# Sink exponentials of a windowed attention: from two fp16 parts in the DMA transposes to one fp32 block turned on TensorE

## The chip, the cores and the metric

The kernel runs on one core of a Trainium2 chip. The metric is the device time of one execution in microseconds (us), the median over several runs. The profile is one more execution, recorded instruction by instruction; its times count from its first instruction.

## What is computed

Three layers follow each other. The change is in the first, an attention with a window of 128 keys and 4 sink keys that every query may see; 2 batches, 8 heads, 768 positions, 64 values per head:

```
scores = scale * np.matmul(q, k.transpose(0, 1, 3, 2))
is_sink = pos[None, :] < int(n_sink)
in_window = (rel >= 0) & (rel < int(window))
scores = np.where(is_sink | in_window, scores, -1000000000.0)
a = np.exp(scores - np.max(scores, axis=-1, keepdims=True))
a = a / (np.sum(a, axis=-1, keepdims=True) + 1e-09)
return np.matmul(a, v).astype(np.float32)
```

Its output, 1536 rows of 512, goes through eight experts (two matrix products each, weighted by normalised gates) and then through a layer with `h * cos(h)`. These two fill most of the time.

## The kernel before

Products are made from fp16 pairs: a value x is stored as a high part `hi` and the rest `lo = x - hi`, and three matmuls give hi·hi, hi·lo and lo·hi.

**Units.** The attention is cut into 48 units, numbered k = 0 to 47: a batch (24 units each), one of four pairs of heads p, and one of six tiles i of 128 queries. Within a pair of heads, units are summed in groups that share one PSUM tile: two groups of three tiles for the first three pairs, three groups of two tiles for the last. Each unit passes through the engines like this:

- `scores(k)` (L533, TensorE): two fp32 matmuls, one per head. 260 columns are 128 keys of the tile before, 4 sink keys and 128 keys of the own tile (132 for the first tile). They go into one ring of four PSUM banks, so two units' scores fit.
- `top(k)` (L545, VectorE, two instructions and two reads of the maximum), then `nm` (L549, VectorE): mask, row maximum, and the bias of the exponential.
- `expo(k)` (L563, ScalarE) and `high(k)` (L574, ScalarE): exponentials, and their fp16 high part of the window's columns.
- `low(k)` (L579, GpSimd): the low part of the window's columns. The eight sink columns (two heads, four sinks) are split on VectorE: L582 makes the high part, L584, one unit later, the low part. They lie in block 0 of the unit's nine blocks of 128 columns.
- `turn(k)` (L589, queue of SyncE): a DMA transposes the nine blocks (five for the first tile).
- `values(k)` (L601, L606, TensorE): two matmuls of 130 columns with block 0 and the sinks' V in two parts (`vs`), then six or twelve matmuls of 65 columns with the other blocks.
- `norm(k)` at the end of a group (L615 to L618, VectorE).

**Order.** Every engine runs its instructions in the order in which the program issues them. That order is set by a hand-written table of ticks: `put(t, every, steps)` puts steps at ticks, `run(n)` issues those of tick n, and `late` holds steps for the start of the next tick. Unit k's scores are at tick 2k (2k+4 for the second batch), its `low` five ticks after, its `values` thirteen ticks after. Work that shares these ticks is placed by the `put` lines that the diff touches: loading V and splitting it (`prep_v`, L187, L189, L190), the sinks' V (`sinks`, L477 on TensorE and L478 on VectorE), loading and scaling the first expert's weights (`w_load`, `w1_split`, L170 for the maxima, L128 to L161 for the scale), and from tick 37 the turning of finished rows into the experts' operand (`x_operand`, L183, L184, L204 to L206, L212). The first batch's ticks end at 66; the second batch's 60 ticks are spread over the first expert's first pass.

Of the kernel before, what the change touches and what calls it, by code (L numbers as in the profile page):

```python
# [10 lines left out]
F32 = mybir.dt.float32  # L11
# [29 lines left out]
def kernel(  # L41
# [263 lines left out]
    def attention():  # L305
# [28 lines left out]
        a16s, ats = Ring(parts16[:, n] for n in range(3)), Ring(parts16[:, n] for n in range(3, 7))  # L334
        more = W2S[0].rearrange("p a b w -> p (a b w)")[:, 3 * 1792:3 * 1792 + 18 * 128].rearrange("p (n a w) -> p n a w", a=9, w=128)
# [4 lines left out]
        for b, home in ((0, HH), (1, W2S[1])):  # L340
            h = home.rearrange("p a b w -> p (a b w)")
            n, n2 = 2 * NP * NT * 2 * DV, 2 * NP * 2 * DV
            vh[b] = h[:, 0:n].rearrange("p (l a t g d) -> p l a t g d", l=2, a=NP, t=NT, g=2)
            vs[b] = h[:, n:n + n2].rearrange("p (l a g d) -> p l a g d", l=2, a=NP, g=2)
# [74 lines left out]
        rep = res.tile([128, 128], F16, name="rep")  # L419
        bm = res.tile([128, 2], F32, name="bm")  # L420
        b2 = res.tile([128, 2], F32, name="bm2")

        def sink_consts():
            for t in a16s.parts:
                nc.gpsimd.memset(t[:, 0, :], 0.0)
            nc.gpsimd.memset(rep, 0.0)
            r = rep[:, 0:4 * NS].rearrange("p (g s) -> p g s", s=NS)
            nc.gpsimd.memset(r, 1.0)
            sel(r, [(0, 1, [[0, 4], [-1, NS]]), (0, -1, [[0, 4], [1, NS]])], 0.0)
            for g, t in enumerate((bm, b2)):  # L430
                nc.gpsimd.memset(t, 1.0)
                o = 2 * g * NS
                sel(t, [(-o, 1, [[-NS, 2]]), (o + NS - 1, -1, [[NS, 2]])], 0.0)
            nc.gpsimd.tensor_tensor(out=bm, in0=bm, in1=b2, op=ALU.add)
# [5 lines left out]
        def prep_v(b, groups):  # L440
# [33 lines left out]
            def sinks(p):  # L474
                ps = ring["l"].next()[:, 0:4 * DV].rearrange("p (l g d) -> p l g d", l=2, g=2)
                for hl in range(2):
                    nc.tensor.matmul(ps[:, hl], rep, vh[b][:, hl, p, 0], start=True, stop=True)  # L477
                nc.vector.tensor_tensor(  # L478
                    out=vs[b][:, :, p], in0=ps, in1=bm[:, None, :, None].to_broadcast([128, 2, 2, DV]), op=ALU.mult)

            def sp(p):
                src = vt[:, p].rearrange("p t (g d) -> p t g d", g=2)
                split(vh[b][:, 0, p, :, :, 0:D], vh[b][:, 1, p, :, :, 0:D], src, sv[:, p:p + 1], by=BY[b][p])

            for n, g in enumerate(groups):
# [5 lines left out]
                for p in range(g.start, g.stop):  # L491
                    steps.append(lambda p=p: sp(p))
                    steps.append(lambda p=p: sinks(p))
            return steps + [ones_col]
# [27 lines left out]
        S_, A_, N_, a16_, at_, X_ = {}, {}, {}, {}, {}, {}  # L522
# [53 lines left out]
        def low(k):  # L576
# [3 lines left out]
            sk = a16_[k][:, 0, 0:4 * NS].rearrange("p (g h s) -> p g h s", g=2, h=2)  # L580
            asn = A.rearrange("p h b w -> p h (b w)")[:, :, 128:TW]
            nc.vector.tensor_copy(out=sk[:, 0], in_=asn)  # L582
            between.append(
                lambda: nc.vector.tensor_tensor(out=sk[:, 1], in0=asn, in1=sk[:, 0], op=ALU.subtract))  # L584

        def turn(k):
# [3 lines left out]
                out=at[:, 0:n], in_=a16_.pop(k)[:, 0:n].rearrange("p a w -> p (a w)"))  # L590

        def values(k):
# [3 lines left out]
            if u == 0:  # L596
                X_[b] = ring["x"].next()[:, 0:n * 2 * DV].rearrange("p (u g d) -> p u g d", u=n, g=2)
            xp = X_[b][:, u]
            nb = 2 if i else 1
            for vi in range(2):  # L600
                nc.tensor.matmul(  # L601
                    xp, at[:, 0, :], vs[b][:, vi, p], start=(vi == 0), stop=False)
            for h in range(2):
                for j in range(nb):
                    for ai, vi in ((0, 0), (0, 1), (1, 0)):
                        nc.tensor.matmul(  # L606
                            xp[:, h], at[:, 1 + 2 * nb * ai + h * nb + j, :], vh[b][:, vi, p, i - (nb - 1) + j, h],
                            start=False, stop=(h == 1 and j == nb - 1 and ai == 1))
# [99 lines left out]
        put(7, 0.5, wl1[:4])  # L708
        p0 = prep_v(0, (slice(0, 1), slice(1, NP)))
# [4 lines left out]
        put(4, 1, p0[-1:])  # L714
        put(8, 1, p0[3:4])
        put(6, 1.0, p0[4:7])
        put(10, 2, p0[7:9])
        put(12, 0.5, p0[9:-1:2])
        put(15, 2.5, p0[10:-1:2])
# [82 lines left out]
    def experts(before):  # L802
# [458 lines left out]
```

## Time and profile before

| | |
|---|---|
| median of three runs | 1353.39 us (1352.38 to 1355.0) |
| the profiled execution's own time | 1356.48 us |
| its span, first to last instruction | 1354.8 us |
| busy over the span: TensorE, VectorE, ScalarE, GpSimd | 94%, 66%, 51%, 47% |
| mean granted clock of TensorE | 0.972 of full speed |

The engines' names in the profile are PE (TensorE matmul), PEld (its weight loads, beside PE), DVE (VectorE), ACT (ScalarE), POOL (GpSimd), SP (SyncE). L12 is line 12 of the kernel before. An operand such as `bank<-hh,parts` is the output and the inputs by the program's names.

### The profile page before, as it was taken

What the parts mean: (1) busy time and instruction counts of PE and PEld (TensorE: products, weight loads), DVE (VectorE), ACT (ScalarE), POOL (GpSimd) and SP (SyncE); (2) the same over time, 40 slices, a digit from 0 to 9 for tenths busy, and PEclk for the clock granted to TensorE, in tenths of its full rate; (3) what the DMA queues carried; (4) which work ended last, traced back from release to release, by engine and by line L of the source; (5) the groups of instructions that cost most, each with busy time, mean ns of one, the idle gap of its engine ahead of it and who ended that gap; (6) DMA issues with size and microseconds to landing.
All of it is one profiled execution on the core that took longest, in us unless ns stands there. A gap on an engine that the chain in (4) does not pass through costs nothing.

```text
span 1354.8 us, 19792 instructions
## 1 busy us (share of the span) xinstructions
PE 1272.4 (94%) x7299; PEld 679.7 (50%) x7299; DVE 894.3 (66%) x1852; ACT 692.4 (51%) x1382; POOL 641.1 (47%) x782
## 2 busy tenths in 40 slices
PE   5666899999999999999999999999999998999998
PEld 3543455454545545455554545555454544545554
DVE  8996852665557753854765485476557589787674
ACT  5665754463636355263534616344461748666452
POOL 4555564522435363253436426342640747377543
PEclk8768899999999999999999999999999998999999
DMA  9888653011111401501231060123102332400001
GB/s 237 172 156 196 148 119 104 1 63 63 63 62 55 148 28 36 187 16 62 76 127 59 12 194 1 62 79 124 62 17 94 55 91 41 103 1 0 32 17 47
DMA packets 140689, 108.78 MB, mean 80 GB/s; under 512 B 100144, under 2 KB 115504, under 8 KB 140592
## 3 DMA queue, kind: packets, MB, share of 16 engines
q1 hardware_dynamic: 126512, 77.22, 22.1%
q0 software_dynamic: 7168, 25.17, 6.1%
q10 hardware_dynamic: 6912, 5.13, 1.4%
q8 instruction: 57, 0.93, 0.3%
q14 instruction: 40, 0.33, 0.1%
HBM read 71.84 MB, written 11.53 MB: 62 GB/s over the span
## 4 chain that ended last, share of the span: by engine, by line
PE 70%; DVE 5%; POOL 5%; issue 3%; ACT 3%; DMA 0%; POOLq 0%; DVEq 0%
PE bank L1035 38%; PE bank L967 28%; PE bank L984 4%; DVE tmp L998 1%; POOL hh L884 1%; POOL S L275 1%; DVE w1o L190 1%; DVE tmp L904 1%; POOL S L274 1%; POOL S L276 1%; DVE tmp L895 1%; ACT tmp L900 1%; POOL S L273 0%; ACT tmp L901 0%; POOL hh L908 0%
## 5 line engine op out<-in xcount | busy, mean ns | idle before, releaser
L1035 PE MATMUL bank<-w2s,hh 128*128 128x512 f16 x2880 | 637.6, 380 | 3.0 <-POOL hh L884 2.2
L967 PE MATMUL bank<-xo,w1o 128*128 128x384 f16 x2688 | 451.1, 328 | 11.8 <-ACT tmp L935 5.2
L1035 PEld LDWEIGHTS <-hh 128*128 128x128 f16 x2880 | 281.1, 98 | 337.7 <-POOL hh L908 4.8
L884 POOL TENSOR_TENSOR hh<-tmp,hh 128x384 f16<-128x384 f32 x256 | 233.0, 929 | 368.7 <-ACT tmp L883 358.7
L967 PEld LDWEIGHTS <-w1o 128*128 128x128 f16 x2688 | 260.8, 98 | 189.2 <-issue 19.6
L935 ACT ACTIVATE tmp<-bank 128x384 f32<-128x384 f32 x192 | 93.4, 487 | 339.8 <-PE bank L967 338.7
L939 DVE TENSOR_TENSOR tmp<-bank,tmp 128x384 f32<-128x384 f32 x192 | 103.7, 553 | 178.7 <-ACT tmp L935 129.3
L984 PE MATMUL bank<-xo,w1o 128*128 128x384 f16 x672 | 119.4, 328 | 4.9 <-ACT tmp L1006 3.8
L1104 DVE SCALAR_TENSOR_TENSOR acc<-bank,PS,acc 128x512 f32<-128x512 f32 x84 | 62.9, 748 | 82.7 <-PE bank L1035 82.3
L882 ACT ACTIVATE hh<-tmp 128x384 f16<-128x384 f32 x192 | 98.9, 515 | 13.2 <-DVE tmp L939 13.2
L883 ACT ACTIVATE tmp<-tmp 128x384 f32<-128x384 f32 x192 | 100.4, 523 | 6.1
L984 PEld LDWEIGHTS <-w1o 128*128 128x128 f16 x672 | 65.7, 98 | 55.7 <-issue 8.2
L906 POOL TENSOR_SCALAR hh<-tmp 128x384 f16<-128x384 f32 x64 | 45.9, 717 | 84.0 <-DVE tmp L904 84.0
L189 ACT ACTIVATE w1o<-S,s 128x1024 f16<-128x1024 f32 x40 | 45.8, 1146 | 76.5 <-POOL S L276 75.8
L167 DVE TENSOR_REDUCE wm<-st 128x1 f32<-128x1024 f32 x68 | 81.5, 1208 | 0.0
L190 DVE SCALAR_TENSOR_TENSOR w1o<-st,s,w1o 128x512 f16<-128x512 f32 x72 | 64.9, 934 | 15.2 <-ACT w1o L189 15.2
L908 POOL TENSOR_TENSOR hh<-tmp,hh 128x384 f16<-128x384 f32 x64 | 67.8, 1059 | 5.3
L190 DVE SCALAR_TENSOR_TENSOR w1o<-S,s,w1o 128x1024 f16<-128x1024 f32 x40 | 55.2, 1380 | 20.4 <-ACT w1o L189 20.4
L998 DVE TENSOR_TENSOR tmp<-bank,tmp 128x384 f32<-128x384 f32 x112 | 59.2, 547 | 12.7 <-ACT tmp L1006 6.4
L190 DVE SCALAR_TENSOR_TENSOR w2s<-st,s,w2s 128x512 f16<-128x512 f32 x72 | 56.4, 797 | 10.3 <-ACT w2s L189 10.1
L189 ACT ACTIVATE w2s<-st,s 128x512 f16<-128x512 f32 x72 | 46.6, 708 | 22.5 <-DVE s L160 22.5
L579 POOL TENSOR_TENSOR parts<-xo,parts 128x512 f16<-128x512 f32 (+1 forms) x38 | 41.0, 1081 | 34.3 <-ACT parts L574 32.0
(187 smaller groups left out, 1313.1 us busy)
## 6 DMA issues: line engine op xcount, KB each, us to landing
st<-in_moe_w_dram SPq DMA_DIRECT2D x56, 512.0 KB, 6.1
f<-in_moe_w_in_dram POOLq DMA_DIRECT2D x16, 512.0 KB, 4.4
f<-in_moe_w_out_dram POOLq DMA_DIRECT2D x16, 512.0 KB, 4.3
w2p<-in_moe_w_dram SPq DMA_DIRECT2D x8, 512.0 KB, 4.2
w_in<-x POOLq DMA_DIRECT2D x16, 256.0 KB, 4.5
w_out<-x POOLq DMA_DIRECT2D x16, 256.0 KB, 4.3
st<-w_out SPq DMA_DIRECT2D x8, 512.0 KB, 5.3
st<-w_in SPq DMA_DIRECT2D x8, 512.0 KB, 6.7
```

The source lines that it names most:

```text
L167: nc.vector.tensor_reduce(out=dst, in_=src, axis=axis, op=ALU.max, apply_absolute_value=True)
L189: nc.scalar.activation(out=hi, in_=src, func=AF.Copy, scale=s)
L190: late.append(lambda: nc.vector.scalar_tensor_tensor(out=lo, in0=src, scalar=s, in1=hi, op0=ALU.mult, op1=ALU.subtract))
L882: nc.scalar.activation(out=hi, in_=src, func=AF.Relu)
L883: nc.scalar.activation(out=dst, in_=src, func=AF.Relu)
L884: nc.gpsimd.tensor_tensor(out=lo, in0=dst, in1=hi, op=ALU.subtract)
L935: nc.scalar.activation(out=t, in_=ps, func=AF.Copy)
L939: nc.vector.tensor_tensor(out=t, in0=ps, in1=t, op=ALU.add)
L967: nc.tensor.matmul(ps, W1O[:, j0 + c, wi, o, kk, :], XO[b][:, kk, o, xi, :], start=(n == 0 and o in (0, 5, 1)), stop=(n == 5), skip_group_ ...
L984: nc.tensor.matmul(ps, W1O[:, j, wi, o, kk, :], XO[b][:, kk, o, xi, :], start=(n == 0), stop=(n == 5))
L998: nc.vector.tensor_tensor(out=t, in0=x, in1=y, op=ALU.add)
L1035: nc.tensor.matmul(ps, HH[:, hi, f, t * 128:(t + 1) * 128], w[:, wi, f, :], start=(f == order[0] and n == 0), stop=(f == order[-1] and n = ...
```

## The change

- `low(k)` no longer splits the sink columns on VectorE. GpSimd copies a unit's eight columns in fp32 into a block that gathers the units of one group (24 columns for three units, 16 for two).
- After a group's last `low`, a new step `sink_turn` turns the block on TensorE (an fp32 transpose into the upper columns of bank 0), and ScalarE copies the result to SBUF.
- The DMA transposes carry eight blocks in place of nine (four in place of five).
- `values` has one fp32 matmul for the whole group in place of two fp16 matmuls per unit; `vs` holds fp32 sinks' V, one copy per unit of a group, zero elsewhere. `sinks(p)` therefore writes 24 rows of 390 in place of 128 rows of 260, sums both parts in PSUM, uses the upper columns of bank 1, and for p = 2 and 3 stands at later ticks.
- V of the first batch's last three pairs is split differently: GpSimd scales it in place (fp32), ScalarE takes the high part, GpSimd the low part. Before, VectorE and ScalarE did it.
- The load of the first expert's weights starts at tick 14 in place of 7, that of the second batch's V at tick 20 in place of 14, and the steps that use them follow.
- `ones` starts as an identity matrix for the transposes and is set to ones later.

```
 def sink_consts():
-    for t in a16s.parts:
-        nc.gpsimd.memset(t[:, 0, :], 0.0)
...
 def sp(p):
     src = vt[:, p].rearrange("p t (g d) -> p t g d", g=2)
+    if b == 0 and p:
+        nc.gpsimd.tensor_scalar(
+            out=vt[:, p], in0=vt[:, p], scalar1=sv[:, p:p + 1], scalar2=None, op0=ALU.mult)
+        late.append(lambda: split(
+            vh[b][:, 0, p, :, :, 0:D], vh[b][:, 1, p, :, :, 0:D], src, None, nc.gpsimd))
+        return
...
 def low(k):
...
-    sk = a16_[k][:, 0, 0:4 * NS].rearrange("p (g h s) -> p g h s", g=2, h=2)
-    asn = A.rearrange("p h b w -> p h (b w)")[:, :, 128:TW]
-    nc.vector.tensor_copy(out=sk[:, 0], in_=asn)
-    between.append(
-        lambda: nc.vector.tensor_tensor(out=sk[:, 1], in0=asn, in1=sk[:, 0], op=ALU.subtract))
+    _, u, n = sums[k]
+    if u == 0:
+        sk_[0] = asks.next()[:, 0:2 * n * NS]
+    nc.gpsimd.tensor_copy(
+        out=sk_[0].rearrange("p (u h s) -> p u h s", u=n, h=2)[:, u],
+        in_=A.rearrange("p h b w -> p h (b w)")[:, :, 128:TW])
+    if u == n - 1:
+        late.append(lambda: sink_turn(k, sk_[0], 2 * n * NS))
+
+def sink_turn(k, sk, rows):
+    ps = BANK[0][0:rows, 384:512]
+    nc.tensor.transpose(ps, sk, ones)
+    def out():
+        sk_[k] = turns.next()[0:rows]
+        nc.scalar.activation(out=sk_[k], in_=ps, func=AF.Copy)
+    late.append(out)
...
 def values(k):
...
     if u == 0:
+        sk = sk_.pop(k + n - 1)
+        nc.tensor.matmul(X_[b], sk, vs[b][0:2 * n * NS, p % 2, 0:n], start=True, stop=False)
...
-    for vi in range(2):
-        nc.tensor.matmul(xp, at[:, 0, :], vs[b][:, vi, p], start=(vi == 0), stop=False)
...
-put(7, 0.5, wl1[:4])
+put(14, 0.5, wl1[:4])
...
-put(12, 1.5, wl1[4:])
-put(28, 2.75, w1_split(0, st, range(1)))
-put(14, 2.0, [lambda p=p: load_v(1, p) for p in range(NP)])
+put(20, 1.5, wl1[4:])
+put(31, 2.75, w1_split(0, st, range(1)))
+put(20, 2.0, [lambda p=p: load_v(1, p) for p in range(NP)])
```

The order of the instructions shows where the new work stands. First GpSimd's queue around units 4 and 5, before (L579 is `low`):

```order
L472 MEMSET hh 128x48 x2
L579 TENSOR_TENSOR parts<-xo_70,parts 128x256 [waits Activation_49]
L579 TENSOR_TENSOR parts<-xo_70,parts 128x512 [waits Activation_49] x2
L579 TENSOR_TENSOR w2s_72<-xo_70,w2s_72 128x512 [waits Activation_49] x2
L579 TENSOR_TENSOR parts<-xo_70,parts 128x512 [waits Activation_49,Pool_49]
```

And the same place of the change, from unit 3's `low` on (L582 is now `low`, L586 the copy of the sink columns, L483 the scaling of V, L184 its low part):

```order
L582 TENSOR_TENSOR w2s_72<-xo_70,w2s_72 128x512 [waits Activation_49]
L586 COPY parts<-xo_70 128x8
L483 TENSOR_SCALAR acc_75<-acc_75,sv_171 128x768 [waits DMAHW0_49,DVE_49]
L483 TENSOR_SCALAR acc_75<-acc_75,sv_171 128x768 [waits DMAHW1_49]
L582 TENSOR_TENSOR w2s_72<-xo_70,w2s_72 128x512 [waits Activation_49]
L586 COPY parts<-xo_70 128x8
L483 TENSOR_SCALAR acc_75<-acc_75,sv_171 128x768 [waits DMAHW2_49]
L184 TENSOR_TENSOR hh<-acc_75,hh 128x12x64 [waits Activation_49] x3
L582 TENSOR_TENSOR parts<-xo_70,parts 128x512 [waits Activation_49]
L586 COPY parts<-xo_70 128x8
```

Two scalings now stand ahead of unit 4's `low`, and a third scaling and three low parts ahead of unit 5's.

TensorE's queue ahead of unit 8's scores, before (L477 is `sinks(1)`, the last two rows the scores of unit 8):

```order
L477 LDWEIGHTS rep
L477 MATMUL bank_85<-hh,rep 128x130 [waits Activation_49]
L477 LDWEIGHTS rep
L477 MATMUL bank_85<-hh,rep 128x130 [waits DVE_49]
L533 MATMUL bank_78<-xo_70 128x260 [waits DVE_49]
L533 MATMUL bank_79<-xo_70 128x260 [waits DVE_49]
```

And of the change (L473 is `sinks(1)`, L595 the transpose of the block of units 3 to 5, L536 unit 8's scores):

```order
L473 LDWEIGHTS rep [waits DVE_49]
L473 MATMUL bank_79<-hh,rep 24x130 [waits Activation_49]
L473 LDWEIGHTS rep
L473 MATMUL bank_79<-hh,rep 24x130 [waits Pool_49]
L595 MATMUL bank_78<-ones,parts 24x128 [waits Pool_49]
L536 MATMUL bank_78<-xo_70 128x260
L536 MATMUL bank_79<-xo_70 128x260 [waits DVE_49]
```

The transpose waits for GpSimd and stands ahead of the scores of the unit three after the group's last; so it does in every group.

## Rows read from the trace of the kernel before

**Rows 1.** Busy time of each engine in five stretches of the span, with clock and DMA.

```profile
0.00:106.00 106.00, 61.80 (x473) 45.59 (x473) 94.74 (x362) 64.03 (x138) 55.23 (x98) 0.77 0.92 187
106.00:113.00 7.00, 2.31 (x9) 0.80 (x8) 0.00 (x0) 1.76 (x5) 1.35 (x2) 0.50 1.12 303
113.00:156.00 43.00, 32.12 (x294) 18.68 (x293) 36.84 (x107) 27.11 (x56) 26.40 (x29) 0.90 0.76 172
156.00:185.00 29.00, 26.25 (x279) 15.65 (x278) 22.91 (x82) 24.31 (x49) 16.11 (x17) 0.94 0.56 114
185.00:1355.00 1170.00, 1149.96 (x6252) 598.94 (x6250) 739.80 (x1302) 575.23 (x1136) 542.02 (x638) 1.00 0.22 65
```

**Rows 2.** Timeline of VectorE around units 11 and 12: start, duration, instruction.

```profile
41.37 0.16 DVE L582 CAST w2s<-xo 128x8 f16<-128x8 f32 x1
41.44 0.42 DVE L545 CUSTOM_DVE_ANT_0 xo<-bank,msk 128x260 f32<-128x260 f32 x1
...
42.14 0.16 DVE L584 TENSOR_TENSOR w2s<-xo,w2s 128x8 f16<-128x8 f32 x1
42.26 0.17 DVE L549 TENSOR_SCALAR nm<-mx 128x2 f32<-128x2 f32 x1
...
43.28 1.08 DVE L582 CAST parts<-xo 128x8 f16<-128x8 f32 x1
```

**Rows 3.** Timeline of GpSimd over the same time.

```profile
43.19 1.15 POOL L579 TENSOR_TENSOR parts<-xo,parts 128x512 f16<-128x512 f32 x1 [2.25 <-issue]
```

**Rows 4.** Busy time of line L582 alone (VectorE) in two stretches.

```profile
0.00:106.00 106.00, 9.51 (x30) 0.77 0.92 187
106.00:185.00 79.00, 8.09 (x18) 0.88 0.72 162
```

**Rows 5.** The same of line L584.

```profile
0.00:106.00 106.00, 10.55 (x29) 0.77 0.92 187
106.00:185.00 79.00, 7.26 (x19) 0.88 0.72 162
```

**Rows 6.** The same of line L549.

```profile
0.00:106.00 106.00, 7.10 (x31) 0.77 0.92 187
106.00:185.00 79.00, 2.75 (x17) 0.88 0.72 162
```

**Rows 7.** Groups of VectorE's instructions, 0 to 215 us: busy, mean ns.

```profile
L190 DVE SCALAR_TENSOR_TENSOR hh<-acc,sv,hh 128x768 f16<-128x768 f32 x4 | 4.0, 1018 | 0.1
L478 DVE TENSOR_TENSOR hh<-bank,bm 128x260 f16<-128x260 f32 x4 | 1.7, 418 | 1.2 <-PE bank L477 1.2
```

**Rows 8.** Groups of GpSimd's instructions, 0 to 215 us.

```profile
L579 POOL TENSOR_TENSOR parts<-xo,parts 128x512 f16<-128x512 f32 x32 | 36.9, 1156 | 28.3 <-ACT parts L574 26.0 <-issue 2.3
L579 POOL TENSOR_TENSOR parts<-xo,parts 128x256 f16<-128x256 f32 x6 | 4.1, 676 | 6.0 <-ACT parts L574 6.0
L206 POOL TENSOR_TENSOR T<-acc,T 128x128 f32<-128x128 f32 x6 | 2.7, 454 | 0.5
L392 POOL TENSOR_SCALAR_AFFINE_SELECT msk<-msk 128x4 f32<-128x4 f32 x4 | 0.8, 193 | 0.3
```

**Rows 9.** A one-input instruction of GpSimd, over the whole span (the page's groups).

```profile
L906 POOL TENSOR_SCALAR hh<-tmp 128x384 f16<-128x384 f32 x64 | 45.9, 717 | 84.0 <-DVE tmp L904 84.0
```

**Rows 10.** Timeline of VectorE: V's scale, and the first `top` of units 8 and 17.

```profile
24.85 0.17 DVE L456 COPY sv<-s 128x3 f32<-128x3 f32 x1
...
31.94 0.42 DVE L545 CUSTOM_DVE_ANT_0 xo<-bank,msk 128x260 f32<-128x260 f32 x1
...
56.87 0.42 DVE L545 CUSTOM_DVE_ANT_0 xo<-bank,msk 128x260 f32<-128x260 f32 x1
```

**Rows 11.** Timeline of TensorE: scores of the first batch, values, scores of unit 46.

```profile
42.57 1.12 PE L533 MATMUL bank<-xo,xo 128*128 128x260 f32 x4
...
126.42 0.28 PE L601 MATMUL bank<-w2s,parts 128*128 128x130 f16 x2
126.54 0.53 PE L606 MATMUL bank<-w2s,parts 128*128 128x65 f16 x12
...
176.68 0.71 PE L533 MATMUL bank<-xo,tmp 64*128 64x260 f32 x4
```

**Rows 12.** Timeline of GpSimd: `low` of unit 43.

```profile
176.95 1.15 POOL L579 TENSOR_TENSOR parts<-xo,parts 128x512 f16<-128x512 f32 x1
```

More of the change, by code (lines that the diff above doesn't have):

```diff
@@ L334, in attention @@
         a16s, ats = Ring(parts16[:, n] for n in range(3)), Ring(parts16[:, n] for n in range(3, 7))
+        asks = Ring(parts16[:, n, 0].bitcast(F32) for n in range(3))
+        turns = Ring([TMP.rearrange("p a b -> p (a b)")[:, 4096 + S:4096 + S + 128], carve(128)])
         more = W2S[0].rearrange("p a b w -> p (a b w)")[:, 3 * 1792:3 * 1792 + 18 * 128].rearrange("p (n a w) -> p n a w", a=9, w=128)
@@ L415, in attention @@
                 blk(snk, [(128 * i - window, 1, -1)])
-        rep = res.tile([128, 128], F16, name="rep")
-        bm = res.tile([128, 2], F32, name="bm")
-        b2 = res.tile([128, 2], F32, name="bm2")
+        G = 2 * U3
+        rep = res.tile([128, G * NS], F16, name="rep")
+        bm = res.tile([128, G], F32, name="bm")
         def sink_consts():
-            for t in a16s.parts:
-                nc.gpsimd.memset(t[:, 0, :], 0.0)
[L426 to L434, printed above, removed]
+            nc.gpsimd.memset(rep, 1.0)
+            sel(rep.rearrange("p (g s) -> p g s", s=NS), [(0, 1, [[0, G], [-1, NS]]), (0, -1, [[0, G], [1, NS]])], 0.0)
+            nc.gpsimd.memset(bm, 1.0)
+            sel(bm, [(0, 1, [[-NS, G]]), (NS - 1, -1, [[NS, G]])], 0.0)
         siv, rv = {}, {}
@@ L490, in prep_v @@
                     steps.append(common)
[L491 to L494, printed above, removed]
+                steps += [lambda p=p: sp(p) for p in range(g.start, g.stop)]
+            return steps, ones_col, [lambda p=p: sinks(p) for p in range(NP)]
         swg = []
@@ L589, in turn @@
             nc.sync.dma_start_transpose(
[L590 removed]
+                out=at[:, 1:n], in_=a16_.pop(k)[:, 1:n].rearrange("p a w -> p (a w)"))
         def values(k):
@@ L607, in values @@
                             xp[:, h], at[:, 1 + 2 * nb * ai + h * nb + j, :], vh[b][:, vi, p, i - (nb - 1) + j, h],
-                            start=False, stop=(h == 1 and j == nb - 1 and ai == 1))
+                            start=False, stop=(u == n - 1 and h == 1 and j == nb - 1 and ai == 1))
         def norm(k):
@@ L713, in attention @@
         put(6, 1, p0[2:3])
[L714 to L719, printed above, removed]
-        put(26, 1, [prep_gate])
-        put(12, 1.5, wl1[4:])
-        put(28, 2.75, w1_split(0, st, range(1)))
-        put(14, 2.0, [lambda p=p: load_v(1, p) for p in range(NP)])
-        p1 = prep_v(1, (slice(0, NP),))
-        put(24, 2.5, p1[-1:] + p1[:-1])
+        put(4, 1, [c0])
+        put(8, 1, k0[:1])
+        put(6, 1.0, p0[3:6])
+        put(10, 2, p0[6:8])
+        put(12, 0.5, p0[8:])
+        put(15, 1, k0[1:2])
+        put(26, 1, [prep_gate])
+        put(20, 1.5, wl1[4:])
+        put(31, 2.75, w1_split(0, st, range(1)))
+        put(20, 2.0, [lambda p=p: load_v(1, p) for p in range(NP)])
+        p1, c1, k1 = prep_v(1, (slice(0, NP),))
+        put(27, 2.3, [c1, *p1])
+        put(52, 7, k1[:2])
+        for p in range(2, NP):
+            put(turned[(p - 1) * NT - 1] + 1, 1, k0[p:p + 1])
+            put(turned[KB + (p - 1) * NT - 1] + 1, 1, k1[p:p + 1])
         def run(n):
@@ L1157, in experts @@
         put(T0 + 15, 1, [lambda: put(10, 1, [probabilities()])])
+        put(T0 + 20, 1, [lambda: nc.gpsimd.memset(ones, 1.0)])
         for n, f in enumerate(sinkhorn()):
@@ L1228 @@
                 channel_multiplier=cm)
+        nc.gpsimd.tensor_copy(out=ones, in_=eye)
         experts(attention())
```

19 lines of the change are left out of this document (9 added, 10 removed).

## The prediction

> **What bounds the kernel now.** I read the stretches first [rows 1]. From 185 us on TensorE is busy 1150 of 1170 us at full clock: nothing that the change touches lies there, so a gain or a loss must come from the first 185 us. Those have three parts. *Stage A*, 0 to 106 us, is the first batch's attention (scores of units 0 to 29): VectorE is busy 94.7 us of 106, TensorE 62, ScalarE 64, GpSimd 55. VectorE sets the pace. From 106 to 113 us VectorE does nothing and TensorE 2.3 us: the first expert waits for its operand's last transposes. The change leaves that as it is. *Stage C*, 113 to 185 us, is the second batch's attention between the first expert's products. Up to 156 us VectorE has 36.8 of 43 us and TensorE 32.1, each often waiting for the other; after that TensorE has 26.3 of 29 us and sets the pace.
>
> Next the instructions that go. Undisturbed, L582 and L584 take 0.16 us each, and the next instruction starts 0.07 and 0.11 us later [rows 2]: 0.18 us per unit is all that they cost by themselves. But another L582 took 1.08 us. It began at 43.28 us, in the middle of GpSimd's L579, which ran from 43.19 to 44.34 us, and ended with it [rows 2, 3]. So VectorE stands still while GpSimd finishes, and most of the two lines' time is this wait.
>
> **What the change takes from VectorE in stage A.** L582 and L584 are busy 9.51 + 10.55 = 20.1 us in 59 instructions [rows 4, 5]. Undisturbed they would be 59 x 0.16 = 9.4, so 10.6 us are waits for GpSimd; with 30 units x 0.18 = 5.4 us of their own, 16.0 us go. How much of the wait moves on to the next instruction that can meet GpSimd, L549 behind the maxima? Now it follows L584, which has done the waiting for it: 7.10 / 31 = 0.23 us against 0.17 undisturbed [rows 2, 6]. The bounds are that no more wait moves to it, and that all 10.6 us do. I take the chance of meeting a busy GpSimd: it is busy 55.2 of 106 us in pieces of about 1.15 us [rows 1, 8], so an instruction that comes at any time waits 0.52 x 1.15 / 2 = 0.30 us. That is 0.24 more per L549, 30 x 0.24 = 7.2 us. It leaves 16.0 - 7.2 = 8.8 us. V's split takes three L190 of 1.02 us off VectorE, 3.1 us [rows 7]. The sinks' V (L478, 0.42 us) grows to 390 columns, at most 0.63 by columns, six times in the stage, and two of them leave it [rows 7]: 6 x 0.21 against 0.84, nothing in sum. The ceiling of stage A is 11.9 us.
>
> **What eats it.** The GpSimd order puts two scalings of V ahead of unit 4's `low`, and a third one and three low parts ahead of unit 5's; behind unit 5's copy wait TensorE's new transpose and, in its queue, the scores of unit 8. Prices: L483 has one input of 768 columns. L906 with 384 takes 0.72 us [rows 9]; its bounds are 0.72 (width free) and 1.43 (in proportion), and I take 1.3. L184 at 768 columns: 0.68 us at 256 and 1.16 at 512 make 0.48 per 256, so 1.64 [rows 8]. The copy of eight columns lies between the 0.19 us of a 4-column select and the 0.45 of a 128-column subtraction [rows 8]; I take 0.2. V's scale is ready at 24.85 us [rows 10], some 0.5 us earlier without the lines removed ahead of it. From 24.4: 3 x 1.3 + 3 x 1.64 + two `low` of 1.16 + two copies = 11.5, so 35.9 us. The transpose has 128 fp32 columns where a score matmul has 260 in 0.56 us [rows 11]: 0.28. The first score matmul follows: unit 8's maximum starts at 36.7 us, not at 31.94 [rows 10], 4.8 us late, while VectorE has little to do. After that TensorE works off what queued behind the transpose: per unit 1.12 for scores, 0.53 for values [rows 11], a third of the new matmul and transpose (0.84 + 0.28; 390 and 128 fp32 columns by the same row), 2.0 us at full clock and 2.6 at the stage's 0.77 [rows 1]. For the nine units to unit 17 that is 18 to 23 us, which gives 54.9 to 60.1 us where it was 56.87 [rows 10]. I take no gain and no loss there: the first 57 us keep nothing of their share. What is left is the share of units 17 to 29, 13 / 30 x 8.8 = 3.8 us. **Stage A: 4 us shorter.**
>
> **Stage C.** L582 and L584 are 8.09 + 7.26 = 15.4 us in 37 instructions [rows 4, 5]: 9.4 of waits and 18 x 0.18 = 3.2 of their own. L549 waits for nothing now (2.75 / 17 = 0.16 us [rows 6]); GpSimd is busy 43.9 of 79 us [rows 1], so by the same chance it takes over 18 x 0.32 = 5.7 us. That leaves 6.9 us. It counts only where VectorE is the pace, 43 of 72 us: 4.1 us. TensorE gets more work. A group of three gains 0.84 + 0.28 us and loses six L601 of 0.06 us (two of them take 0.12, from 126.42 to 126.54 [rows 11]): +0.76. A group of two gains 0.56 + 0.28 and loses 0.24: +0.60. Of the seven groups of this stage, those that end with units 41, 43, 45 and 47 fall after 156 us, where TensorE is idle only 2.75 us [rows 1]: 0.76 + 3 x 0.60 = 2.6 us longer. The three earlier ones lie in 10.9 us of idle time; without it they would cost 2 us. The transposes can also make TensorE wait for GpSimd: unit 43's `low` ended at 178.1 us, and with its copy the transpose could start at 178.3, but TensorE was at the scores behind it at 176.68 [rows 11, 12], 1.6 us to wait. VectorE running earlier shrinks that; I take 1 us. **Stage C: 4.1 - 2.6 - 1 = 0.5 us shorter.** The later loads, the smaller transposes and the late `ones` cost nothing: ScalarE's maxima of the weights lie in a stage where it is busy 64 of 106 us, and without that room their four instructions would delay the exponentials by as much as they last.
>
> **Sum.** 4 + 0.5 = 4.5 us. The profiled execution would go from 1356.48 to 1352.0 us; it lay 3.1 us above the median of the runs. Against the median the forecast is 1353.4 - 4.5 = **1348.9 us**, with 1345 to 1351 as this case's own range. A measurement of this kernel can tell about 0.2% (2.7 us) from no change.
>
> **Rivals.** *The wait only moves* (no change). If L549 takes over all of the waits, by 10.6 and 9.4 us, VectorE keeps only the instructions' own time: 13 / 30 x 5.4 = 2.3 us in stage A and 0.6 x 3.2 = 1.9 in stage C, less the 3.6 us that TensorE pays: about 1352.8 us. For it: L549 is of the same kind as a waiting L582, and GpSimd gets six more long pieces and 48 copies. Against it: today three instructions of a unit meet GpSimd, and then one. The Trainium skill states this lock (SBUF — State Buffer, "Who interferes with whom"): whichever of VectorE and GpSimd issues first has their shared port pair for its whole instruction, and the other stands still; tensor_scalar is among the instructions that can need it. The L582 that ended with GpSimd's L579 [rows 2, 3] agrees.
>
> *TensorE is tied to GpSimd* (slower). The place is the transpose ahead of the scores of unit k + 3. It decides from the point where GpSimd's copy ends later than VectorE is ready for the next scores. If scalings, low parts and copies keep GpSimd behind, the 4.8 us of unit 8 are never worked off, and in stage C each of the last four turns waits the 1.6 us found at unit 43: 4.8 - 3.8 + 6.4 + 2.6 - 4.1 = 5.9 us slower, 1359.3 us. For it: TensorE now has a wait on GpSimd in every group where it had none, and scores feed everything else. Against it: VectorE's own lateness is what made `low` late, and it gets shorter.
>
> *The early jam is small* (much faster). With L483 at its lower bound (3 x 0.6 us less), TensorE at full clock (54.9 less that 1.8 us, against 56.87: 3.8 us) and half the assumed move of waits (7.2 and 5.7 halved), stage A gives 3.8 + 13 / 30 x 12.4 = 9.2 us and stage C 5.8 - 2.6 = 3.2: 12.4 us in all, 1341 us.
>
> **Chances.** The forecast 0.42, the wait that moves 0.22, the tie 0.18, the small jam 0.18. Faster by over 0.2%: nearly all of the forecast and the small jam, 0.56; within it 0.26; slower 0.18. The range leaves out about a tenth on each side: from a little past the small jam, 1339 us, to somewhat short of the tie, 1357.5.
>
> **What would show it.** Right: L549 at some 0.4 us each, the idle time of VectorE between 25 and 37 us with unit 8's first `top` near 36.7 us, unit 17's near 57 us, TensorE's first expert product some 4 us earlier, and the first time from which TensorE stays busy at about 180 us. Wrong: unit 8 no later than before (L483 or the jam mispriced), L549 near 0.2 us (waits vanish), or TensorE idle ahead of the transposes in stage C for more than 3 us in sum. Most of all the forecast hangs on how much of the early delay is made good by unit 17.

## The result, and the profile after

The changed kernel takes 1368.43 us (median of four runs, 1365.43 to 1370.18) where the kernel before takes 1354.01 beside it: ratio 1.0105, interval 1.0085 to 1.0126. It is 14.4 us slower; the forecast was 4.5 us faster. The profiled execution took 1368.41 us, with a span of 1366.7 (1354.8 before), so 11.9 us of the loss can be followed in the two traces. The kernel before was profiled in an execution of 1356.48 us, 2.5 above its median, so that differences of spans read low by about as much.

The stretches of the changed kernel, as in [rows 1]: length, then busy time of TensorE, its weight loads, VectorE, ScalarE and GpSimd, granted clock, DMA share, GB/s.

```profile
0.00:106.00 106.00, 63.85 (x416) 42.80 (x417) 78.62 (x267) 60.46 (x135) 66.22 (x115) 0.74 0.87 168
106.00:113.00 7.00, 4.89 (x23) 2.59 (x20) 6.61 (x25) 4.49 (x11) 4.26 (x6) 0.50 0.73 110
113.00:156.00 43.00, 33.06 (x239) 16.98 (x240) 26.92 (x76) 23.69 (x53) 25.66 (x35) 0.80 0.85 191
156.00:185.00 29.00, 25.65 (x263) 14.30 (x260) 21.66 (x72) 22.93 (x50) 15.71 (x22) 1.00 0.61 128
```

VectorE is busy 16 us less in the first 106 us and yet is not done sooner: between 106 and 113 us, where it did nothing before, it now works 6.6 us. It waits. Its timeline at unit 8 and unit 17, where `top` (now L548) began at 31.94 and 56.87 us [rows 10]:

```profile
38.48 0.43 DVE L548 CUSTOM_DVE_ANT_0 xo<-bank,msk 128x260 f32<-128x260 f32 x1 [5.17 <-ACT xo L599]
...
63.80 0.43 DVE L548 CUSTOM_DVE_ANT_0 xo<-bank,msk 128x260 f32<-128x260 f32 x1 [1.58 <-PE bank L536]
```

GpSimd's timeline ahead of unit 8 shows the two scalings of V, `low` of unit 4 and its copy, the third scaling, the three low parts, and `low` of unit 5 with its copy:

```profile
22.99 4.41 POOL L483 TENSOR_SCALAR acc<-acc,sv 128x768 f32<-128x768 f32 x2 [3.00 <-DVE siv L452]
27.37 1.15 POOL L582 TENSOR_TENSOR w2s<-xo,w2s 128x512 f16<-128x512 f32 x1
28.47 0.19 POOL L586 COPY parts<-xo 128x8 f32<-128x8 f32 x1
28.64 2.20 POOL L483 TENSOR_SCALAR acc<-acc,sv 128x768 f32<-128x768 f32 x1
30.80 4.68 POOL L184 TENSOR_TENSOR hh<-acc,hh 128x768 f16<-128x768 f32 x3
35.45 1.15 POOL L582 TENSOR_TENSOR parts<-xo,parts 128x512 f16<-128x512 f32 x1
36.54 0.19 POOL L586 COPY parts<-xo 128x8 f32<-128x8 f32 x1
```

TensorE's timeline over the same time, and at unit 17:

```profile
32.45 0.27 PE L473 MATMUL bank<-hh,rep 128*24 128x130 f16 x1 [5.37 <-POOL hh L184]
36.78 0.39 PE L595 MATMUL bank<-ones,parts 128*24 128x128 f32 x1 [4.06 <-POOL parts L586]
36.96 1.94 PE L536 MATMUL bank<-xo 128*128 128x260 f32 x4
...
62.37 0.39 PE L595 MATMUL bank<-ones,parts 128*24 128x128 f32 x1 [2.17 <-POOL parts L586]
62.55 1.08 PE L536 MATMUL bank<-xo,xo 128*128 128x260 f32 x2
```

The transpose L595 waits until GpSimd's copy ends at 36.73 us, and unit 8's scores (L536) come right behind it. The first head's score ends at 38.04 us, and then the maximum waits once more, for ScalarE's copy of the turned block, which reads the same bank 0:

```profile
38.07 0.27 ACT L599 ACTIVATE xo<-bank 24x128 f32<-24x128 f32 x1 [4.80 <-PE bank L536]
```

TensorE's waits from 6 to 113 us, largest first (total, times, longest); before, none of them was for GpSimd:

```profile
PE bank L595 <- POOL parts L586: 13.9, 4, 5.2
PE bank L536 <- DVE xo L371: 5.8, 1, 5.8
PE bank L149 <- DVE w1o L142: 5.6, 2, 5.0
PE bank L473 <- POOL hh L184: 5.4, 1, 5.4
```

All comparisons of places below use one reading: the start of a unit's first `top` on VectorE's timeline, less the same start in the kernel before. For the changed kernel it is +6.5 us at unit 8, +6.9 at 17, +9.1 at 24, +9.5 at 30 and +9.6 at 47. The loss arises in stage A; stage C neither adds nor returns anything, and 2.3 us more follow behind unit 47: from its first `top` to the end of the attention's last values matmul 15.8 us pass, 13.5 before. TensorE's granted clock up to unit 30 was 0.73 (0 to 113.80 us) against 0.77 before (0 to 104.26 us); no run separates what this costs from the waits.

### The profile page after: what moved, and what is told of

It reads as the page before. It is cut to its first block, busy times and chain, and to the rows that moved or that the text cites. A ratio compares the mean times of both kernels' runs of the same rounds, so it can differ in the third digit from the quotient of the medians.

```text
span 1366.7 us, 19653 instructions
## 1 busy us (share of the span) xinstructions
PE 1286.7 (94%) x7257; PEld 679.8 (50%) x7257; DVE 879.0 (64%) x1752; ACT 695.9 (51%) x1401; POOL 661.9 (48%) x827
## 4 chain that ended last, share of the span: by engine, by line
PE 68%; POOL 7%; DVE 6%; ACT 4%; issue 4%; DMA 1%; POOLq 0%; DVEq 0%; ACTq 0%
PE bank L1056 35%; PE bank L988 28%; PE bank L1005 4%; DVE tmp L1019 2%; POOL hh L905 1%; DVE w1o L190 1%; DVE tmp L925 1%; POOL T L204 1%; DVE tmp L916 1%; POOL hh L929 1%; DMA xo<-xs 1%; POOL S L275 1%; POOL S L274 1%; POOL S L276 1%; ACT tmp L921 0%
## 5 line engine op out<-in xcount | busy, mean ns | idle before, releaser
L1005 PEld LDWEIGHTS <-w1o 128*128 128x128 f16 x672 | 66.0, 98 | 57.4 <-issue 10.1
L190 DVE SCALAR_TENSOR_TENSOR w2s<-st,s,w2s 128x512 f16<-128x512 f32 x72 | 56.5, 798 | 10.3 <-ACT w2s L189 10.1
L582 POOL TENSOR_TENSOR parts<-xo,parts 128x512 f16<-128x512 f32 (+1 forms) x38 | 43.0, 1132 | 31.1 <-ACT parts L577 27.4
```

Of the source, the lines that this page charges most:

```text
L190: late.append(lambda: nc.vector.scalar_tensor_tensor(out=lo, in0=src, scalar=s, in1=hi, op0=ALU.mult, op1=ALU.subtract))
L1005: nc.tensor.matmul(ps, W1O[:, j, wi, o, kk, :], XO[b][:, kk, o, xi, :], start=(n == 0), stop=(n == 5))
```

## The experiments

Every run was timed beside the kernel before. "us" is the ratio less one, times 1354; the next columns are the starts of units 8, 30 and 47 and the span, less before, in the profiled execution (span of before: 1354.8). Where the runs of a kernel scatter, that execution can differ from the median by 3 us or so (14 most: its runs reach from 1352.95 to 1357.42, and 1353.08 was profiled). A difference of two runs' ratios is uncertain by 2 to 4 us, taken from their two intervals.

| run | what | ratio, 95% interval | us | 8 | 30 | 47 | span |
|---|---|---|---|---|---|---|---|
| | the change | 1.0105 [1.0085, 1.0126] | +14.2 | +6.5 | +9.5 | +9.6 | +11.9 |
| 1 | transposes behind the scores | 1.0055 [1.0036, 1.0074] | +7.4 | +5.0 | +2.8 | +2.2 | +4.6 |
| 2 | V split as before | 1.0062 [1.0040, 1.0084] | +8.4 | -1.1 | +3.9 | +3.6 | +5.8 |
| 3 | V's sink matmul later | 1.0115 [1.0090, 1.0139] | +15.6 | +6.6 | +10.5 | +12.0 | +14.9 |
| 4 | before, later loads alone | 1.0027 [1.0009, 1.0045] | +3.7 | -1.1 | +2.1 | +2.4 | +3.0 |
| 5 | before, V's split alone | 1.0058 [1.0035, 1.0080] | +7.9 | +1.9 | +5.4 | +5.7 | +6.3 |
| 6 | sinks alone | 1.0038 [1.0025, 1.0052] | +5.1 | +0.7 | +1.2 | +0.9 | +4.5 |
| 7 | 6, transposes behind scores | 1.0019 [1.0002, 1.0035] | +2.6 | -0.6 | -0.1 | -1.5 | +2.2 |
| 8 | 7, copy ahead of `low` | 1.0022 [1.0006, 1.0038] | +3.0 | +1.6 | +1.8 | +1.9 | +4.1 |
| 9 | before less L582, L584 | 0.9940 [0.9923, 0.9957] | -8.1 | -1.0 | -5.8 | -8.1 | -7.2 |
| 10 | 7 less TensorE's sinks | 0.9934 [0.9917, 0.9951] | -8.9 | -1.7 | -3.1 | -7.8 | -7.9 |
| 11 | before, V's loads later | 1.0006 [0.9997, 1.0015] | +0.8 | +0.0 | -1.2 | -1.2 | -0.9 |
| 12 | before, L582 to ScalarE, L584 to GpSimd | 0.9935 [0.9920, 0.9951] | -8.8 | -1.7 | -5.9 | -10.1 | -9.1 |
| 13 | before, W1 later | 1.0044 [1.0029, 1.0059] | +6.0 | -1.0 | +5.8 | +5.4 | +5.1 |
| 14 | 7, sink matmul in fp16 | 1.0006 [0.9996, 1.0016] | +0.8 | -0.6 | -3.0 | -3.8 | -3.4 |
| 15 | 5, high part later | 1.0054 [1.0039, 1.0069] | +7.3 | -3.0 | +5.3 | +6.5 | +6.7 |
| 16 | 12 with 15 | 0.9973 [0.9964, 0.9982] | -3.7 | -3.5 | +1.8 | -4.4 | -4.0 |
| 17 | 14 less ScalarE's copies | 0.9981 [0.9968, 0.9993] | -2.6 | -0.7 | -3.5 | -6.2 | -5.9 |
| 18 | 5, only scalings on GpSimd | 1.0050 [1.0034, 1.0065] | +6.8 | +3.8 | +2.1 | +2.2 | +2.6 |

**The changed kernel, one part undone (1, 2, 3).** Run 1:

```diff
-                late.append(lambda: sink_turn(k, sk_[0], 2 * n * NS))
+                sk = sk_[0]
+                late.append(lambda: late.append(lambda: sink_turn(k, sk, 2 * n * NS)))
```

> The changed kernel with one edit: the transpose of the sinks' exponentials is queued one step later on TensorE, behind the scores of unit k+3 instead of ahead of them (ScalarE's copy of it one step later too). The changed kernel takes 14.4 us more than the one before. Theory A (the scores are tied to GpSimd through the transposes ahead of them): in the first 113 us the transposes wait 13.9 us for GpSimd's copy in four places; they now have two scores' time (5 to 6 us) more, so most of this goes and with it 8 to 11 us of the loss: 3 to 7 us slower than before, unit 24's maximum some 2 us late instead of 9. Theory B (GpSimd's late split of V does the harm by itself: its work delays the low parts and the matmul of V's sink rows): unit 8 stays 6 us late and the time stays at 10 us or more above before. Theory C (VectorE meets more of GpSimd's work in their common lock, and loses time there): 12 us or more above before, since nothing of that changes.

Half of the loss goes, most of it behind unit 17. Unit 8 stays 5 us late, and TensorE's timeline shows the transpose (here L596) still waiting for GpSimd, but with the scores of unit 8 ahead of it at 32.26:

```profile
32.26 2.10 PE L536 MATMUL bank<-xo 128*128 128x260 f32 x4
36.39 0.39 PE L596 MATMUL bank<-ones,parts 128*24 128x128 f32 x1 [2.03 <-POOL parts L586]
```

VectorE's timeline of the same run:

```profile
36.93 0.43 DVE L548 CUSTOM_DVE_ANT_0 xo<-bank,msk 128x260 f32<-128x260 f32 x1 [4.01 <-PE bank L596]
```

The scores were done at 34.4 us, but their maximum waited for the transpose: both lie in PSUM bank 0, in different columns, so it is the bank that ties them, not the data. The Trainium skill (PSUM — Partial Sum Buffer, "PSUM bank collisions raise a hardware error") gives the reason: two engines must not be in one bank on the same partitions at once, whatever the columns, so a program has to guard the bank with semaphores, and not single columns of it. The wait of 4.01 us agrees with it. So theory A holds for half, and the order in TensorE's queue is not the only tie.

Run 2: `if b == 0 and p:` in `sp` never taken.

> The changed kernel with one edit: batch 0's V is split by VectorE and ScalarE as in the kernel before, in the changed kernel's order. GpSimd loses three scalings of 2.2 us and three low parts of 1.6 us, 11.4 us. Theory A (tie by the transposes): unit 8 is in time, but the later waits of the transposes (62, 88 and 93 us) stay: 6 to 10 us slower than before. Theory B (the split does the harm): unit 8 is in time and so is what follows, 0 to 4 us slower than before, and VectorE's 3 us for the split return. Theory C (lock): 4 us of the loss go at most, 10 us slower.

As theory A has it: unit 8 is 1.1 us early, and from unit 16 to 24 the start goes from -3.0 to +3.5.

Run 3: `put(15, 1, k0[1:2])` becomes `put(22, 1, k0[1:2])`.

> The changed kernel with one edit: the matmul that spreads V's sink rows for the second pair of heads, which waited 5.4 us for GpSimd's low part of V at 27 to 32 us, is queued seven steps later on TensorE, when that part has long been written. If this wait is what holds the scores of unit 8, unit 8 comes 2 to 4 us earlier and the time falls to 8 to 12 us above before. If the transpose behind it holds them (theory A), it waits for the same low(5) and copy: unit 8 stays at 37 to 39 us and the time at 13 to 15 us above before.

Theory A again: L473's wait of 5.4 us is gone, and the transpose takes it over.

```profile
36.82 0.39 PE L595 MATMUL bank<-ones,parts 128*24 128x128 f32 x1 [9.91 <-POOL parts L586]
```

**The kernel before, with the later loads (4, 11, 13).** Run 4 takes the new steps of W1 and of batch 1's V, run 11 V's alone, run 13 W1's alone:

```diff
-        put(7, 0.5, wl1[:4])
+        put(14, 0.5, wl1[:4])
-        put(12, 1.5, wl1[4:])
+        put(20, 1.5, wl1[4:])
-        put(28, 2.75, w1_split(0, st, range(1)))
+        put(31, 2.75, w1_split(0, st, range(1)))
```

> The kernel before with the later steps alone: the first expert's W1 is loaded and its maxima taken seven and eight steps later, its first split three steps later, batch 1's V loaded six steps later and prepared three steps later. The prediction put this at nothing: within 1.5 us of before. A rival theory, that these steps now fall where VectorE or ScalarE has no room, makes it 3 to 6 us slower, with units 24 to 30 late by as much and the first 20 units in time.

> The kernel before with batch 1's V alone loaded six steps later and prepared three steps later; the first expert's W1 stays in its steps. Theory: all the later loads together cost 3.7 us because V's 1.5 MB now fly at 40 to 60 us beside the turning transfers, and TensorE waits 9.1 us for these: then 2 to 4 us slower here too, with such waits. Rival: the later maxima of W1 on ScalarE do it: within 1 us of before.

> The kernel before with the first expert's W1 alone loaded seven steps later, its maxima eight and its first split three steps later; batch 1's V in its steps. If W1 does what the later loads together cost: 2 to 4 us slower than before. If the cost needs both, W1 and V side by side in flight: within 1.5 us.

The forecast's "nothing" is wrong, and so is my theory of run 11 that V's loads do it: W1 does. In run 13 TensorE, ScalarE and VectorE wait for a turning transfer at unit 14. ScalarE's maxima of W1 ran before that, from 33.6 to 42.9 us, and units 9 to 13 were still 0.6 to 3.0 us early; unit 14 is 4.0 us late. DMA issues between 38 and 52 us, first of the kernel before, then of run 13 (the last number is the median from issue to landing):

```profile
parts<-parts SPq DMA_TRANSPOSE x4, 4.9
parts<-w2s SPq DMA_TRANSPOSE x2, 5.1
```

```profile
parts<-parts SPq DMA_TRANSPOSE x3, 6.6
parts<-w2s SPq DMA_TRANSPOSE x2, 11.0
```

TensorE's waits of run 13 from 38 to 55 us; before, it waits for no transfer there:

```profile
PE bank L601 <- DMA parts<-parts: 6.6, 3, 4.2
PE bank L601 <- DMA parts<-w2s: 1.8, 1, 1.8
```

W1's four loads of 512 KB were issued by 16.2 us before and took 6.9 us to land (median), ahead of batch 1's V. In run 13 they are issued from 23.85 to 27.2 us, with V's first load between them, and take 9.2; V's next ones follow at 33.69, 38.48 and 40.47 us, and the turning transfers land late among all these. With V's loads moved on as well (run 4) the loss is 3.7 us, a difference within the noise. Run 13 moved W1's loads together with its maxima and first split, so that the transfers do it is read from these waits and not tested alone.

**The kernel before, with V's split on GpSimd (5, 15, 18).** Run 5 takes over the branch of `sp` from the diff of the change; the sink rows' matmuls move from step 15 to 19, and V's load for batch 1 from 14 to 20. Run 15 appends ScalarE's high part three steps later (the sink rows' matmuls from step 23, batch 1's V loaded from 22 and prepared from 28), run 18 gives the low parts `nc.vector`.

> The kernel before with the split of batch 0's V for the last three pairs of heads moved to GpSimd, as in the changed kernel (the matmuls of their sink rows four steps later, batch 1's V loaded six steps later, since both now wait for GpSimd). Theory A (the split harms only through TensorE's new wait for GpSimd): without transposes ahead of the scores unit 8 is in time, VectorE's 3 us for the split show as a gain, and the time is 1 to 3 us below before. Theory B (GpSimd's 11.4 us ahead of the low parts of units 4 and 5 do the harm by themselves, through late values and VectorE's wait in the common lock): 3 to 6 us above before, with unit 8 or 9 late by as much.

> The kernel before with V's split on GpSimd, as run alone (8 us slower), but ScalarE's high part and GpSimd's low part of V three steps behind the scaling instead of none, and what needs V's parts (the sink rows' matmuls, batch 1's V) some steps later too. If ScalarE's wait for the scaling, with exponentials queued behind it, does the harm: 4 to 8 us less, from 3 us faster to 3 us slower than before. If GpSimd's 11.4 us ahead of the low parts do it wherever they stand: 5 to 9 us slower as before.

> The kernel before with only the scaling of batch 0's V for the last three pairs on GpSimd (6.6 us there); the low parts, 4.8 us on GpSimd, go back to VectorE, which has them with two inputs and no scale. With both on GpSimd it is 7 to 8 us slower than before. If the harm goes with GpSimd's time: 4 to 5 us slower. If the low parts ahead of units 5 and 6 are the harm: within 2 us of before. If the scalings are, which VectorE's and ScalarE's next steps wait for: 6 to 8 us slower.

There is no transpose on TensorE in run 5, and it loses 7.9 us all the same: theory B. ScalarE's longest wait of run 5 (20 to 62 us), then TensorE's two longest:

```profile
ACT hh L183 <- POOL acc L484: 5.3, 2, 4.0
...
PE bank L149 <- DVE diag L142: 9.2, 2, 8.5
PE bank L607 <- DMA parts<-w2s: 6.9, 1, 6.9
```

ScalarE's queue stands behind the scaling, with the exponentials of units 5 and 6 in it. Run 15 takes that away: unit 8 is 3.0 us early, yet 5.3 us late at unit 30. So that wait is not what counts. Run 18 says that the low parts on GpSimd aren't either, as far as its scattered runs tell. TensorE's wait of 8.5 us for the scale of W1 (L142) is run 5's alone: it is 3.9 us in run 15 and 2.1 in run 18, as before, and they lose as much. What all three share is V scaled on GpSimd, batch 1's V loaded later for it, and waits of TensorE for turning transfers between 40 and 62 us, where it had none before (6.9 us in run 5, 5.7 in 15, 4.6 in 18). The later load by itself cost 0.8 us, within the noise (run 11). Which of these does the rest is open.

**The sinks alone (6, 7, 8).** The changed kernel with the edits of 2 and the old steps of all loads (6), with that of 1 added (7), and with GpSimd's copy placed ahead of `low` (8).

> The changed kernel with V split and the loads in their steps as before, so that only the handling of the sinks' exponentials is changed. If the three parts add up (tie about 7 us, V's split 6, later loads 3, and 2 us of gain from what VectorE no longer does), it is 4 to 6 us slower than before. If the later loads cost nothing beside the tie, 7 to 9 us slower, as with V's split alone undone. If the forecast's sum for the sinks by themselves were right (VectorE's share less TensorE's work), 2 to 4 us faster.

> The same as the sinks alone, with the transposes one step later, behind the scores of unit k+3. If the tie's 7 us go here too and the parts add up: 1 to 4 us faster than before. If VectorE's lock with GpSimd takes back what VectorE gave up (the maxima's small instruction at 0.4 us each) and TensorE's added work counts: within 1.5 us of before or slower. Unit 24's maximum at 84 to 87 us (86.1 before).

> The same again, with GpSimd's copy of the eight exponentials ahead of the unit's low part instead of behind it: the copy needs only the exponentials, so the transpose no longer waits for ScalarE's high part and GpSimd's low part. If waits for the copy are left in the kernel with late transposes, 1 to 3 us less than that one; if the late transposes already meet a finished copy, the same within 1 us, or 1 us more, since the low part and the transfer behind it come a copy later.

Even without the other parts, and with the transposes out of the way, the sinks' new handling gains nothing. Run 8 gains nothing on 7.

**Where VectorE's gain goes (9, 10, 14, 17).** Run 9 deletes L582 and L584 from the kernel before. Run 10 edits run 7, run 14 makes the last of these edits only, and run 17 takes ScalarE's `out` off run 14:

```diff
-                late.append(lambda: late.append(lambda: sink_turn(k, sk, 2 * n * NS)))
...
-                nc.tensor.matmul(X_[b], sk, vs[b][0:2 * n * NS, p % 2, 0:n], start=True, stop=False)
+                nc.tensor.matmul(X_[b], at[:, 1, :], vh[b][:, 0, p, 0:n], start=True, stop=False)
```

> The kernel before with VectorE's two small instructions (L582, L584) left out and nothing in their place; the sinks' exponentials then count as zero. This is the forecast's first term by itself. The forecast's reckoning: 8.8 us in the first stage and 4.1 in the third, 9 to 13 us faster than before, with the maxima's small instruction at 0.4 us each. A rival, that the waits in them only move and that other engines set the order's pace too: 0 to 4 us faster.

> The kernel with the sinks alone changed and late transposes, less TensorE's part in them: no transposes and no copies out of PSUM, and in place of the fp32 matmul of 390 columns one in fp16 on data at hand (the sinks don't count). VectorE and GpSimd do what they did. If TensorE's added work (busy 12.7 us more in all than in the kernel before) is what eats VectorE's gain, 5 to 9 us less than with it, so 3 to 6 us faster than before. If it is VectorE's waits for GpSimd, 2 to 4 us less, from what follows unit 47 alone: the same as before within 1.5 us.

> The kernel with the sinks alone changed and late transposes, with one edit: the fp32 matmul of 390 columns is replaced by one in fp16 on data at hand (the sinks don't count); the transposes and ScalarE's copies stay. Left out of both, the kernel was 11 us faster. TensorE's time for them is 18 x (0.92 + 0.34) us at full clock, so by time the matmul is 0.7 of it: 7 to 9 us less than with the fp32 matmul, 4 to 7 us faster than before. If the transposes' waits and ScalarE's copies are what matters, 1 to 4 us less: from 2 us faster than before to 1 us slower.

> The kernel with the sinks' matmul in fp16 on data at hand and late transposes, less ScalarE's 18 copies of the transposes out of PSUM (nothing reads these there). Transposes and GpSimd's copies stay. If the waits for ScalarE's copy harm (between units 31 and 47 VectorE waits 8.2 us for it, since the transposes lie in the bank of the scores): 3 to 6 us less, 3 to 6 us faster than before. If TensorE's wait for GpSimd's copies (8.3 us there) and its time for the transposes harm: within 1.5 us of what it was, the same as before.

Runs 9 and 10 settle it. Without the two instructions the kernel is 8.1 us faster (run 9). With GpSimd's copies, the smaller transfers and one fp16 matmul per group it is 8.9 (run 10): the copies cost nothing that shows. The waits do move on to L549, as the forecast had it. Its busy time in run 9, to be set beside [rows 6]:

```profile
0.00:106.00 106.00, 13.40 (x31) 0.77 1.00 203
106.00:185.00 79.00, 5.37 (x17) 0.90 0.71 155
```

TensorE's part of the sinks with ScalarE's copies, from run 10 to run 7, costs 11.5 us. The page's busy time of TensorE over the whole span, first of run 10, then of run 7:

```profile
PE 1271.6 (94%) x7221; PEld 675.7 (50%) x7221; DVE 883.5 (66%) x1756; ACT 692.8 (51%) x1382; POOL 650.9 (48%) x821
```

```profile
PE 1287.4 (95%) x7257; PEld 679.3 (50%) x7257; DVE 881.4 (65%) x1756; ACT 696.4 (51%) x1400; POOL 648.4 (48%) x821
```

TensorE has 15.8 us more to do, but that is not what most of the 11.5 us are. The busy time of the one matmul per group (L617), first in fp32 (run 7), then in fp16 (run 14): TensorE, weight loads, clock, DMA share, GB/s.

```profile
0.00:200.00 200.00, 19.76 (x36) 6.67 (x36) 0.85 0.77 163
```

```profile
0.00:200.00 200.00, 6.80 (x18) 1.87 (x18) 0.85 0.80 166
```

With 13 us of TensorE's time gone the kernel is 1.8 us faster by the ratios, which is within the noise, and 5.6 by the spans, where run 14's profiled execution lay 3 us below its median. So TensorE's idle time covers the greater part of that work. ScalarE's copies are 3.4 us by the ratios (14 to 17) and 2.5 by the spans, the transposes with their waits 6.3 (17 to 10) and 2.0; in run 17 TensorE waits 11.0 us for GpSimd's copies ahead of them. How the 11.5 us divide exactly stays open. That ScalarE's copies cost something both say, and the trace shows how. VectorE's waits from 113 to 200 us in run 7, where L600 is ScalarE's copy out of bank 0:

```profile
DVE xo L548 <- ACT tmp L600: 6.4, 3, 2.4
DVE xo L548 <- ACT xo L600: 4.7, 2, 3.7
```

**A version that beats both (12, 16).** Run 12 leaves TensorE's work and the transfers as before, and gives the two instructions to engines with room:

```diff
             nc.scalar.activation(out=blocks(k, 0), in_=A_[k][:, :, 0:nb, 0:128], func=AF.Copy)
+            sk = a16_[k][:, 0, 0:4 * NS].rearrange("p (g h s) -> p g h s", g=2, h=2)
+            nc.scalar.activation(out=sk[:, 0], in_=A_[k].rearrange("p h b w -> p h (b w)")[:, :, 128:TW], func=AF.Copy)
...
-            nc.vector.tensor_copy(out=sk[:, 0], in_=asn)
-            between.append(
-                lambda: nc.vector.tensor_tensor(out=sk[:, 1], in0=asn, in1=sk[:, 0], op=ALU.subtract))
+            nc.gpsimd.tensor_tensor(out=sk[:, 1], in0=asn, in1=sk[:, 0], op=ALU.subtract)
```

> The kernel before with the same two small instructions taken by other engines: the fp16 high part of the sinks' exponentials by ScalarE behind the unit's high part, the low part by GpSimd behind the unit's low part; TensorE's work and the steps stay. If VectorE's two instructions are worth 9 us or more by themselves: 4 to 9 us faster. If their waits only move, and ScalarE and GpSimd become as late by the work they take (some 0.2 and 0.3 us in each of 48 units): from 1 us faster to 4 us slower.

> The kernel with the sinks' fp16 parts on ScalarE and GpSimd (8.8 us faster than before), with V's split on GpSimd and its high part three steps later added. If the late high part removes the harm, VectorE's 3 us add up: 9 to 12 us faster than before. If GpSimd is too full by now: 3 to 7 us faster, so slower than without the split.

Run 12 is 8.8 us faster than before, as fast as leaving the instructions out. With V's split on GpSimd on top of it (16) 5 us of that are lost again.

## Why the prediction was wrong

- **What VectorE gives up.** Right in kind, too large in size. L549 took the waits at 13.40 / 31 = 0.43 us each in stage A (0.4 forecast). The gain was 5.8 us by unit 30 against 8.8 forecast, and 8.1 by unit 47 against 12.9 (run 9). VectorE's busy time up to unit 30 fell from 93.07 (0 to 104.26 us) to 86.54 us (run 9, 0 to 98.51), 6.5 of the 16.0 that went: L549 took up 6.3, and other instructions of VectorE some 3, which the sum did not have. "The wait only moves" was not the case.
- **TensorE's part and its ties: the first step that failed.** The sum had 2.6 us for TensorE's work in stage C, 1 us there for the transposes' waits, nothing for ScalarE's copies, and in stage A a third of 1.12 us for each of nine units, which was to be worked off by unit 17. Measured together they cost 11.5 us (7 less 10). The durations were right (0.27 to 0.42 us for a transpose against 0.28; TensorE's busy time went from 1272.4 to 1286.7 us), and the long matmul is not what was mispriced: it costs 1.8 us by the ratios and 5.6 by the spans. The rest, some 5 to 10 us, goes by runs 14 and 17 with the short work that ties engines together: transposes that wait for GpSimd in TensorE's queue, and maxima that wait for transposes and ScalarE's copies in bank 0.
- **Unit 8.** Forecast at 36.7 us, it came at 38.48. GpSimd's scaling takes 2.20 us, not 1.3, above the upper bound of 1.43; the three make 2.7 us, and V was scaled from 22.99 instead of 24.4. The low parts took 1.59 and the copy 0.19, as forecast. From the copy's end to the maximum 1.75 us passed, not the 0.84 of the sum: TensorE's granted clock was 0.50 of full speed from 36.78 to 38.91 us, the lower of its two levels, where the first head's score took 1.08 us and not 0.56, and the maximum waited for ScalarE's copy (L599), which the forecast did not have.
- **"No gain and no loss at unit 17": the second step that failed.** Unit 17 was 6.9 us late. Half of the jam had been worked off by unit 16, which was 3.0 us late; then the transpose that waited for GpSimd at 62 us brought it back. V's split costs some 6 us with the rest of the change (the change less run 2) and 7.9 us alone (run 5), so the harm is not only the transposes' wait that I had set it down to.
- **The tie.** Its mechanism is real: putting the transposes behind the scores gives back 6.8 us with the rest in place (run 1), and 2.5 us, within the noise, with the sinks alone (6 to 7). I had its place in stage C, 1.6 us in each of four groups; it lies in stage A (62, 88 and 93 us), where GpSimd's first-expert work stands ahead of `low` and copy. The rival's 1359.3 us was too low by 9, since the other costs came on top. What I had held against it, that VectorE's lateness is what makes `low` late, does not hold where GpSimd's own queue is what is late.
- **The later loads: the third step that failed.** Put at nothing on ScalarE's room; they cost 3.7 us alone, and the traces show the waits at transfers, not at ScalarE's maxima (run 13).
- **Stage C.** 0.5 us shorter forecast, unchanged from unit 30 to 47, then 2.3 us lost up to the last values matmul. There the forecast had TensorE's work, 2.6 us.

From the kernel before, the spans chain up to the whole: the two instructions go, GpSimd's copies and smaller transfers come, -7.9 (run 10); TensorE's and ScalarE's part with late transposes, +10.1 (7); transposes ahead of the scores, +2.3 (6); later loads, +1.3 (2); V's split, +6.1 (the change). That makes 11.9 us. By the ratios the same steps are -8.9, +11.5, +2.5, +3.3 and +5.8, 14.2 us, each uncertain by 2 to 4 us, so only the first two and the last are clear of the noise. The shares depend on the order: the loads alone are 3.0 us by the span, the transposes with the rest in place 7.3.

The Trainium skill's rule on the port pair (SBUF — State Buffer, "Who interferes with whom") says that where a VectorE instruction takes the ports that it shares with GpSimd, the one of the two that issues first has them for its whole instruction. Where the waits of L582 and L584 went in run 9, to VectorE's next instruction, agrees with it: 0.23 to 0.43 us per L549. The loss does not lie there: VectorE's busy time, which holds such waits, is 879.0 us in the changed kernel and 880.6 in run 9.

## What to carry to other kernels

Price a new piece of work by what it ties together, not by its length alone: here 13 us of matmul time cost between 2 and 6 us, and 18 short transposes and 18 copies, 6 and 5 us of work, between 5 and 10 us (runs 7, 14, 10). Look for the engine whose result is wanted last (run 12 used ScalarE and GpSimd, behind instructions that they had anyway). Before an in-order queue gets an operand from another engine, ask how late that engine runs at its worst place, and what else lies in the same PSUM bank. A load that is put off meets other transfers: look at what flies in the new stretch, not only at who needs the data.

## What the runs showed of the hardware

- GpSimd's scaling with one input, fp32 to fp32, took 2.20 us for 128x768; its subtraction with two inputs and fp16 output took 1.59 for the same shape, and a scaling of 384 columns with fp16 output 0.72 [rows 9]. Whether the fp32 output does it was not tried.
- Eight columns cost ScalarE 0.19 us and GpSimd 0.20 (medians of run 12's L576 and L584), so the 48 pairs of them are some 19 us of work, and run 12 is no slower than run 9, which leaves them out.
- Two turning transfers issued between 38 and 52 us took 11.0 us to land in the median (run 13) where two took 5.1 before, with hardly more bytes moved, 2.79 MB against 2.71 between 38 and 52 us, and 3.80 against 3.19 in the 14 us ahead.
